# A planned transformer block: ScalarE planned at a shorter pitch, ten x tiles transposed by DMA, slabs and wo loaded after them

## The chip, the cores and the metric

The kernel runs on one core of a Trainium2 chip. The time is device microseconds of one launch. Before the change it is 1136.66 us, the median of three runs from 1135.99 to 1137.84.

## What is computed

One transformer block on 2048 tokens of width 1024, in bf16: attention with 32 query heads of 32 columns that share one key head and one value head, then a gated feed-forward of width 3584.

```python
x = A_x                                   # (1, 2048, 1024)
n = layernorm(x)                          # (x - m) / sqrt(v + eps)
q = heads(n @ wq); k = n @ wk; v = n @ wv # q: 32 heads of 32; k, v: 32 columns
p = softmax(q @ k.T * 32 ** -0.5)
h = x + merge(p @ v) @ wo
m = layernorm(h)
out = h + (sigmoid(m @ w_gate) * (m @ w_up)) @ w_down
```

## The kernel before, in words

**A planner writes the order.** The kernel is straight-line code for five in-order engines. While it is built, `Plan` (from line 40) simulates the engines with fixed costs and lists each engine's instructions in the order in which its simulation starts them; `emit` then writes these lists with semaphore waits. On the chip the order never changes: an instruction that is ready later than planned holds everything behind it on its engine. `op` (58) adds an instruction; for PE it is placed at once, for the others `step` (94) takes the earliest that can start, by priority where several can. Costs planned: a matmul of n columns n/2.4 + 2.4 ns, 97 ns for each change of PE between dense, row-tiled ("row": scores) and column-tiled ("col": PV, SUM) matmuls (`SWITCH`, 151), ACT `t_act` (143), DVE `t_dve` (147), a DMA 450 ns of SP and a landing from a rate and fixed parts (116 to 121). "pace" spaces the weight loads at `PACE_RATE`.

**The stages.** x comes in 16 tiles of 128 tokens into `ring`. Of each tile DVE takes the statistics and subtracts the mean (359), POOL makes 1/std (340 to 346), DVE or ACT scales it into `xn` (`make_norm1`, 363), PE transposes it in eight 128x128 blocks into PSUM (`mk_xT`, 398), and `evac` (257) gives the copy into `xnT`, a part of `zone`, to ACT (266) or DVE (267), whichever is free sooner by the plan. KV groups (438) make keys and values; Q groups (491, 507) make queries, which go through DRAM. When a tile quad of x is scaled, its room in `ring` is given to the first gate and up slabs (`load_next`, 847); a slab is 1024 x 512 of w_gate or w_up, 1 MB in four DMAs. wo is loaded at line 310, after x and wq.

A score visit (`emit_S`, 614) handles one half of a 128-token tile's heads (`hf`, 0 to 31) against 128 keys (`kt`): four S matmuls (row-tiled), then two exps of 128x1024 on ACT (632), which write one slot of 2048 columns. There are 512 visits. The first 32 go over halves 0 and 1 alternately and need the keys of tile after tile as these come. DVE adds the slots of a half up (607); SUM (657) gives the denominators, by DRAM, to all partitions (670, 671); PV (693) multiplies by the values. For halves 0 and 1 (`RAW`) the denominators come from PV-like matmuls with ones. `finish` (678) divides. OP (776) multiplies by wo, DVE adds x (783), takes statistics and normalises (789), and a DMA transposes the result into `hnT` (804).

The feed-forward goes tile by tile: GU groups (gate: tanh on ACT, 919; up: combined on DVE, 925), seven slab pairs a pass, odd passes backwards so that two slab pairs are reused; then D groups (949, four quarters of the width) with w_down, which stays in SBUF as 14 loads (`load_wd`, 472) into `zone`, in the room of xnT and wq. So a wd load waits for the last use of its x block, and the last six wait for all of Q (`wd_after_q`, 485). GU of tile 1 and any D wait for all of Q too.

**How the next PE work is picked** (main loop, from 1001). If a score visit can start and ACT's backlog is below `run`, it goes first, also in the middle of a group. Else the current group goes on. A long group (D, GU, Q) may be set aside for a PV, SUM or OP group. If there is no current group, the first class in `PRIO` (380) with a ready group and a free one of the two PSUM banks is taken; `PRIO_D` (379) takes its place when a D group is due. PV and SUM are let in from row mode, or with few free slots (`in_row`, 654; `pv_few`, `sum_few`).

Of the kernel before, what the change touches and what calls it, by code (L numbers as in the profile page):

```python
# [10 lines left out]
ALU = mybir.AluOpType  # L11

P = 128
DH = 32
LN_EPS_BF16 = 1.0013580322265625e-05
SEM = 75.0


TUNE = dict(nkn=2, few=0, rmin=1000, hmin=3, h0=100, h1=100, hf=1.5, run=1300, sum_few=12, pv_few=1, d_off=0,
            d_a=1, d_b=1, eb=0, eq=0)  # L20

# [18 lines left out]
class Plan:  # L40


    ENG = ("act", "dve", "pool", "sp")
    DMA_RATE = 260.0
    LATE = {"rb": 1000.0, "hT0": 300.0, "hT1": 300.0}
    PACE_RATE = 250.0

# [46 lines left out]
    def step(self, limit):  # L94
        best = None
        for e in self.ENG:
            h = self.heap[e]
            if h:
                s = min(self.start_of(o) for o in h)
                if best is None or s < best[0]:  # L100
                    best = (s, e)
        if best is None or (limit is not None and best[0] > limit):
            return False
        s, e = best
        h = self.heap[e]
        o = min((o for o in h if self.start_of(o) <= s + 1e-9), key=lambda o: (o.prio, o.seq))
        h.remove(o)
        if o.pace and self.pace_free > s:
            s2 = self.pace_free
            prev = [a for a in self.lists["act"][-6:] if a.end <= s2]  # L110
            if prev:
                o.deps.append(prev[-1])
            s = s2
        self.free[e] = s + o.occ
        o.start = s
        if o.nbytes:
            if o.pace:
                self.pace_free = s + o.nbytes / self.PACE_RATE
            go = max(s + 1300.0, self.dma_free)
            self.dma_free = go + o.nbytes / self.DMA_RATE  # L120
            o.end = self.dma_free + 700.0 + self.LATE.get(o.key, 0.0)
        else:
            o.end = s + o.lat
        o.pos = len(self.lists[e])
        self.lists[e].append(o)
        for u in o.users:
            u.ready = max(u.ready, o.end)
            u.missing -= 1
            if u.missing == 0:
                self.heap[u.eng].append(u)  # L130
        o.users = []
        return True
# [10 lines left out]
def t_act(n):  # L143
    return dict(occ=n / 1.2 + 96.0, lat=n / 1.2 + 186.0 + SEM)

# [8 lines left out]
def bass_sequential_preLN__grouped_kv_mqa__glu_gated_glu__prompt_kernel(  # L154
# [12 lines left out]
    Bsz, S, D = A_x.shape  # L167
# [17 lines left out]
    with ExitStack() as es:  # L185
# [58 lines left out]
        def x_sb(t):  # L244
            return x_ring[:, t, :]
# [63 lines left out]
        load_wq(3)  # L309
        wo_ld = dma(lambda: SP.dma_start(wo_sb[:, :, :], A_wo.rearrange("(g p) n -> p g n", p=P)), "wo", D * D * 2, prio=1)  # L310

# [39 lines left out]
        sv1 = {}  # L351
        for tiles in ([0], [1], [2, 3], [4, 5], [6, 7], [8, 9, 10], [11, 12, 13], [14, 15]):
            r = stats(0, tiles, [x_sb(t) for t in tiles], [[x_ld[t]] for t in tiles], 3)
            for t in tiles:
                sv1[t] = r
        xnorm = {}
        xcent = {}
        for t in range(NT):
            xcent[t] = pl.op("dve", lambda t=t: DVE.tensor_scalar(  # L359
                out=x_sb(t), in0=x_sb(t), scalar1=mvr[:, 0, t, 0:1], scalar2=None, op0=ALU.subtract),  # L360
                [sv1[t][0]], prio=2, occ=330, lat=500)

        def make_norm1(t, deps):
            dst, src, sc = xn[:, t % 2, :], x_sb(t), rstd[:, 0, t:t + 1]
            xnorm[t] = evac(lambda: ACT.activation(out=dst, in_=src, func=ACTF.Copy, scale=sc),
                            lambda: DVE.tensor_scalar(out=dst, in0=src, scalar1=sc, scalar2=None, op0=ALU.mult),  # L366
                            1024, [xcent[t], sv1[t][1]] + deps, 1, 3.2, bias=TUNE["eb"])

        make_norm1(0, [])
# [9 lines left out]
        PRIO_D = ["xT", "KV", "Q0", "PV", "SUM", "OP", "hT", "D", "GU", "Q1", "Q"]  # L379
        PRIO = ["xT", "KV", "Q0", "PV", "SUM", "OP", "hT", "Q1", "Q", "GU", "D"]  # L380

# [13 lines left out]

        xT_ev = {}

        def mk_xT(t):
# [6 lines left out]
            def after(b, last):  # L405
# [3 lines left out]
                if t + 2 < NT:  # L409
                    make_norm1(t + 2, [last])  # L410
                    if (t + 2) % 4 == 3:
                        sl = (t + 2) // 4
                        load_next([(ring_u[:, u], [xnorm[2 * u], xnorm[2 * u + 1]]) for u in (2 * sl, 2 * sl + 1)])
                queue_after_xT(t)
                return [xT_ev[t]]
# [172 lines left out]
        late_adds = collections.defaultdict(list)  # L588
        RAW = (0, 1)
        rs_b = h_sb[:, 2, :].bitcast(F32)  # L590
# [23 lines left out]
        def emit_S(v):  # L614
# [23 lines left out]
            if hh == 1 and c % 2 == 1 and kt == NT - 1:  # L638
                pair_last_S[c // 2] = last
                load_q(c // 2 + 2)  # L640
            if kt % 8 == 7:
                if kt == NT - 1 and hf not in RAW:
                    queues["SUM"].append(mk_SUM(hf))
                queues["PV"].append(mk_PV(hf, kt // 8))
                if hf in RAW:
                    queues["PV"].append(mk_PV(hf, kt // 8, True))

        rb_ld = {}
        rs_ev = {}
# [28 lines left out]
        def finish(hf):  # L678

            if hf not in rb_ld or (hf, 1) not in oun_ev:  # L680
                return
            c, hh = hf // 2, hf % 2
            o = oun[:, hf % 2, :]
            r = rs_b if hf == 1 else rb[:, :]
            ot_ev[hf] = pl.op("dve", lambda: DVE.tensor_tensor(
                out=OT[:, 4 * hh:4 * hh + 4, :], in0=o.rearrange("p (a b) -> p a b", a=4),
                in1=r.rearrange("p (a b) -> p a b", a=4), op=ALU.mult),
                [oun_ev[(hf, 1)], op_last.get(c - 1)] + rb_ld[hf], prio=0, occ=600, lat=690)
            if hh == 1:
# [3 lines left out]
        def mk_PV(hf, part, sums=False):  # L693

            kts = range(8 * part, 8 * part + 8)

# [6 lines left out]
            def after(b, last):  # L703
                if sums:
                    r = rs_b if hf == 1 else rb[:, :]
                    if part == 0:
# [3 lines left out]
                    e = pl.op("dve", lambda: DVE.tensor_tensor(out=r, in0=F_ps[:, b, :], in1=r, op=ALU.add),  # L710
                              [last, rs_ev[hf]], prio=0, **t_dve(512))
                    rb_ld[hf] = [pl.op("dve", lambda k=k: DVE.reciprocal(r[:, k * P:(k + 1) * P], r[:, k * P:(k + 1) * P]),
                                       [e], prio=1, occ=P * 8 / 0.96 + 20, lat=P * 8 / 0.96 + 90 + SEM) for k in range(4)]
# [7 lines left out]
                else:  # L721
                    oun_ev[(hf, 1)] = pl.op("dve", lambda: DVE.tensor_tensor(out=o, in0=F_ps[:, b, :], in1=o, op=ALU.add),  # L722
                                            [last, oun_ev[(hf, 0)]], prio=0, **t_dve(512))
                    finish(hf)
                return [oun_ev[(hf, part)]]
# [50 lines left out]
        def mk_OP(t, dc):  # L776
# [19 lines left out]
            def gate():  # L796
                return t in xr_ld and xr_ld[t].end is not None and (t == 0 or (t - 1) in hT_last)
            return Group("OP", atoms, lambda: [ot_ev[2 * t], ot_ev[2 * t + 1], wo_ld], after, gate)

# [145 lines left out]

        ND = 4
        DW = D // ND

        def mk_D(p, t, dq):
# [9 lines left out]
            def after(b, last):  # L959
# [5 lines left out]
                d_ev[t].append(e)  # L965
                if dq % 2 == 1:
                    dc = dq // 2
                    s2 = slice(dc * 512, (dc + 1) * 512)
                    out_dma[(t, dc)] = dma(lambda: SP.dma_start(of[t * P:(t + 1) * P, s2], h_sb[:, t % NHB, s2]),
                                           f"o{t % NHB}{dc}", P * 1024, d_ev[t][-2:], prio=2)  # L970
                if dq == ND - 1 and t + NHB < NT:
                    load_xr(t + NHB)
                return [e]
            return Group("D", atoms, lambda: [hact_ev[(t, ft)] for ft in order[:-8]] + [wd_ld.get(ft) for ft in order[:-8]], after,
                         lambda: q_left[0] == 0)

        d_ev = collections.defaultdict(list)
        for t in range(NT):
            queues["xT"].append(mk_xT(t))

# [20 lines left out]
        while True:  # L1001
# [10 lines left out]
            if 1 in ot_ev and 0 in xr_ld and 2 not in xr_ld:  # L1012
                load_xr(2)
            start_ffn()
            if v < NV:
# [5 lines left out]
                if can_s and run - t < TUNE["run"]:  # L1021
# [3 lines left out]
                    idle = 0  # L1025
                    continue
            else:
                can_s = False
            if cur is not None and not held and cur[0].cls in LONG and known(bank_rel[1 - cur_b], t) and (
                    v >= NV or len(free_slots) <= TUNE["few"] or (len(cur[1]) - cur_i) * max(25.0, cur[1][cur_i][1] / 2.4 + 2.4) >= TUNE["rmin"]):  # L1030

                for cl in ("PV", "SUM", "OP", "hT"):
                    if queues[cl]:
                        gr = queues[cl][0]
# [24 lines left out]
            else:  # L1059
                pick = None  # L1060
                banks = [b for b in range(2) if known(bank_rel[b], t)]
                if banks:
                    pr = PRIO
                    if d_due and len(queues["GU"]) <= d_due[0] + TUNE["d_off"]:
# [135 lines left out]
```

## Time and profile before

| what | us |
|---|---|
| median of the runs | 1136.66 |
| the profiled execution, its own time | 1136.12 |
| its span, first to last instruction | 1134.3 |
| PE busy | 1095.5 (97%) |
| PE weight loads busy | 747.4 (66%) |
| ACT busy | 1033.6 (91%) |
| DVE busy | 834.9 (74%) |
| mean granted TensorE clock | 0.994 |
| DMA moved | 218.13 MB, 192 GB/s mean |

How to read it: busy PE is matmuls in flight, and they overlap, so the engine's real use is read from the distances between starts. ACT's exps overlap too (1035 ns each, but they start closer than that). In rows of the profile "xN" is a count, and what stands in brackets is idle time before an instruction and what ended it. A span is shorter than the execution's own time by what lies around the first and last instruction, here 1.8 us.

### The profile page before, as it was taken

How to read it: one execution, taken by the hardware profiler on the slowest of the kernel's cores; microseconds unless marked ns; L12 is line 12 of the kernel's file. 1: busy time of each engine (PE TensorE's matmuls, PEld its weight loads, DVE VectorE, ACT ScalarE, POOL GpSimd, SP SyncE). 2: the span in 40 equal slices, each digit the busy share in tenths (PEclk: the TensorE clock that was granted, in tenths of full speed). 3: DMA queues.
4: the chain of work that ended last, by engine and by line, in shares of the span. 5: the costliest groups of instructions: out<-in, count | busy, mean ns of one | idle time of the engine just before them, and what ended most of it. 6: DMA issues, size and time to landing. Idle time of an engine off the chain costs nothing.

```text
span 1134.3 us, 34513 instructions
## 1 busy us (share of the span) xinstructions
PE 1095.5 (97%) x15085; PEld 747.4 (66%) x15112; DVE 834.9 (74%) x1042; ACT 1033.6 (91%) x1157; POOL 55.6 (5%) x94
## 2 busy tenths in 40 slices
PE   5999989799999999999999999999999999999999
PEld 4643355467676776767676676767677676667798
DVE  8838987597877767787777877787777778777521
ACT  5899999999999999999999999999999999999410
POOL 4200000010000000000000000000000100000000
PEclk9999999899999999999999999999999999999999
DMA  9423379565766767666667576665847475666783
GB/s 311 146 82 119 98 253 257 176 192 175 194 187 208 213 204 201 182 179 193 196 187 227 153 245 184 180 206 166 255 129 232 144 245 147 213 199 187 241 278 106
DMA packets 231671, 218.13 MB, mean 192 GB/s; under 512 B 34784, under 2 KB 218080, under 8 KB 231520
## 3 DMA queue, kind: packets, MB, share of 16 engines
q1 hardware_dynamic: 231520, 215.92, 63.7%
q8 instruction: 119, 1.95, 0.7%
q14 instruction: 32, 0.26, 0.1%
HBM read 203.55 MB, written 8.11 MB: 187 GB/s over the span
## 4 chain that ended last, share of the span: by engine, by line
PE 87%; ACT 6%; DVE 5%; issue 1%; DMA 1%; POOL 0%; DVEq 0%
PE F_ps L383 74%; PE S_ps L383 13%; ACT Pr L632 5%; DVE st L327 1%; DVE st L329 1%; DVE acc L607 1%; DVE zone L366 1%; DMA ring<-in_B_w_gate_dram 1%; DVE zone L267 1%; DVE ring L359 0%; ACT tnh L919 0%; DVE hact L925 0%; DMA ring<-in_A_x_dram 0%; PE F_ps L401 0%; DVE oun L722 0%
## 5 line engine op out<-in xcount | busy, mean ns | idle before, releaser
L632 ACT ACTIVATE Pr<-S_ps 128x1024 bf16<-128x1024 f32 x1008 | 964.2, 1035 | 20.4 <-PE S_ps L383 11.5
L607 DVE TENSOR_TENSOR acc<-acc,Pr 128x2048 bf16<-128x2048 bf16 x420 | 513.5, 1223 | 103.2 <-ACT Pr L632 91.9
L383 PE MATMUL F_ps<-hnT,ring 128*128 128x128 bf16 x6848 | 440.2, 220 | 3.9 <-issue 1.8
L383 PEld LDWEIGHTS F_ps<-hnT,ring 128*128 128x128 bf16 x6848 | 387.7, 98 | 75.7 <-issue 70.0
L383 PE MATMUL F_ps<-zone,hact 128*128 128x256 bf16 x1792 | 227.8, 273 | 0.0
L383 PE MATMUL S_ps<-QTb,kT 32*128 32x512 bf16 x2048 | 203.2, 387 | 12.3 <-ACT Pr L632 11.2
L383 PEld LDWEIGHTS F_ps<-zone,hact 128*128 128x128 bf16 x1792 | 163.4, 98 | 48.6 <-issue 29.8
L383 PE MATMUL F_ps<-Pr,Vt 128*32 128x512 bf16 x2016 | 132.7, 387 | 1.6 <-DVE r_sb L668 0.6
L383 PEld LDWEIGHTS S_ps<-QTb,kT 32*128 32x128 bf16 x2048 | 51.7, 91 | 115.6 <-ACT Pr L632 46.7
L919 ACT ACTIVATE tnh<-F_ps 128x512 f32<-128x512 f32 x112 | 67.4, 601 | 51.3 <-PE F_ps L383 50.4
L925 DVE SCALAR_TENSOR_TENSOR hact<-tnh,F_ps 128x512 bf16<-128x512 f32 x112 | 76.4, 682 | 45.8 <-PE F_ps L383 43.9
L383 PEld LDWEIGHTS F_ps<-Pr,Vt 128*32 128x32 bf16 x2016 | 45.7, 97 | 59.4 <-issue 18.2
L383 PE MATMUL F_ps<-zone 128*128 128x512 bf16 (+3 forms) x575 | 73.8, 276 | 2.7 <-ACT zone L266 1.4
L383 PE MATMUL F_ps<-wo_sb,OT 128*128 128x512 bf16 x238 | 59.7, 381 | 1.6 <-DVE h_sb L783 0.6
L383 PEld LDWEIGHTS F_ps<-zone 128*128 128x128 bf16 x584 | 40.3, 99 | 29.9 <-issue 8.9
L340 POOL TENSOR_SCALAR zb<-mvb 128x1 bf16<-128x1 bf16 (+2 forms) x24 | 9.1, 381 | 1022.7 <-DVE mvb L336 1022.5
L962 DVE SCALAR_TENSOR_TENSOR h_sb<-F_ps,h_sb 128x256 bf16<-128x256 f32 x64 | 26.9, 420 | 31.2 <-PE F_ps L383 31.0
L607 DVE TENSOR_TENSOR acc<-Pr 128x2048 bf16<-128x2048 bf16 x30 | 35.9, 1198 | 10.3 <-ACT Pr L632 10.2
L383 PEld LDWEIGHTS F_ps<-wo_sb,OT 128*128 128x128 bf16 x256 | 22.5, 98 | 27.7 <-issue 7.2
L722 DVE TENSOR_TENSOR oun<-F_ps,oun 128x512 f32<-128x512 f32 x32 | 22.0, 687 | 24.3 <-PE F_ps L383 24.2
L668 DVE RECIPROCAL r_sb<-F_ps 128x64 f32<-128x64 f32 x30 | 16.7, 556 | 21.9 <-PE F_ps L383 21.7
L783 DVE TENSOR_TENSOR h_sb<-F_ps,h_sb 128x512 bf16<-128x512 f32 x32 | 22.1, 690 | 10.8 <-PE F_ps L383 10.2
(72 smaller groups left out, 333.9 us busy)
## 6 DMA issues: line engine op xcount, KB each, us to landing
ring<-in_B_w_gate_dram SPq DMA_DIRECT2D x312, 256.0 KB, 3.8
ring<-in_B_w_up_dram SPq DMA_DIRECT2D x312, 256.0 KB, 3.9
rb<-r_scratch SPq DMA_DIRECT2D x120, 64.0 KB, 2.3
zone<-in_B_w_down_dram SPq DMA_DIRECT2D x14, 512.0 KB, 4.5
ring<-in_A_x_dram SPq DMA_DIRECT2D x16, 256.0 KB, 6.5
h_sb<-in_A_x_dram SPq DMA_DIRECT2D x16, 256.0 KB, 2.8
out_dram<-h_sb SPq DMA_DIRECT2D x32, 128.0 KB, 3.5
Pr<-in_B_w_up_dram SPq DMA_DIRECT2D x16, 256.0 KB, 4.1
```

The costliest lines, as they stand in the source:

```text
L267: lambda: DVE.tensor_copy(out=out_ap, in_=in_ap))
L327: a = pl.op("dve", lambda s=s, src=src: DVE.bn_stats(st[:, s, 0, :], src[:, 0:512]), dp, prio=prio, occ=600, lat=756, order=[st_user.get(s)])
L329: b = pl.op("dve", lambda s=s, src=src: DVE.bn_stats(st[:, s, 1, :], src[:, 512:1024]), dp, prio=prio, occ=600, lat=756, order=[st_user.ge ...
L383: return lambda: PE.matmul(o, lhsT=l, rhs=r, start=start, stop=stop, **kw)
L607: add_op[(hf, kt)] = pl.op("dve", lambda: DVE.tensor_tensor(out=a, in0=in0, in1=slot, op=ALU.add), dp, prio=6, **t_dve(2048, 1.92))
L632: exps[u] = pl.op("act", lambda i=i, pb=pb: ACT.activation(out=slot[:, i * 1024:(i + 1) * 1024].rearrange("p (a b) -> p a b", a=2), in_=S_ ...
L668: rc = pl.op("dve", lambda: DVE.reciprocal(r_sb[:, :], F_ps[:, b, 0:64]), [last, rd_ld.get(hf - 1)], prio=0, occ=64 * 8 / 0.96 + 20, lat=6 ...
L722: oun_ev[(hf, 1)] = pl.op("dve", lambda: DVE.tensor_tensor(out=o, in0=F_ps[:, b, :], in1=o, op=ALU.add), [last, oun_ev[(hf, 0)]], prio=0, ...
L783: h_ev[(t, dc)] = pl.op("dve", lambda: DVE.tensor_tensor(out=h_sb[:, t % NHB, sl], in0=F_ps[:, b, :], in1=h_sb[:, t % NHB, sl], op=ALU.add ...
L919: box["a"] = pl.op("act", lambda: ACT.activation(out=tnh[:, :], in_=F_ps[:, b, :], func=ACTF.Tanh, scale=0.5), [last, box.get("e")], prio= ...
L925: e = pl.op("dve", lambda: DVE.scalar_tensor_tensor(out=ho, in0=shape(tnh[:, :]), scalar=1.0, in1=shape(F_ps[:, b, :]), op0=ALU.add, op1=A ...
L962: e = pl.op("dve", lambda: DVE.scalar_tensor_tensor(out=h_sb[:, t % NHB, sl], in0=F_ps[:, b, 0:DW], scalar=0.5, in1=h_sb[:, t % NHB, sl], ...
```

## The change

The costs that the planner reckons with: ACT is occupied for n/1.2 + 58 ns by an instruction of n columns, not + 96. A DMA is planned as 1500 ns, its bytes at 270 (not 260) per ns, and 750 ns; extra lateness is 300 for rb, 400 for hT and xt (before 1000 and 300). Weight loads are paced at 280, not 250.

x tiles 0 to 5 go on as before. Tiles 6 to 15 are scaled in place by DVE and transposed by DMA straight into `xnT` (`x_by_dma`). All slabs, and wo, are loaded only after tile 15 has been transposed. Statistics are grouped in pairs.

The order of PE: GU and D stand ahead of Q1 and Q. D waits for all of w_down. GU's gate waits for three of a slab's four DMAs. SUM is let in from row mode or with at most 2 free slots (before 12), PV with 3 (before 1). In column mode, when the next visit is ready within 200 ns, PE waits. The planner's evacuation choice is biased against ACT (`eb` 450, `eq` 1000). Other new keys have values that leave things as they are (`parts=2`, `raw=2`, `nd=4`, and `pc=16`, which is no tile).

```diff
-TUNE = dict(nkn=2, few=0, rmin=1000, hmin=3, h0=100, h1=100, hf=1.5, run=1300, sum_few=12, pv_few=1, d_off=0,
-            d_a=1, d_b=1, eb=0, eq=0)
+TUNE = dict(swait=200, parts=2, raw=2, rl=0, nd=4, pc=16, rate=270, pace=280, xd=6, qf=0, dall=1, wo_late=1,
+            nkn=3, few=2, rmin=700, hmin=1, h0=100, h1=100, hf=1.0, run=900, sum_few=2, pv_few=3, d_off=2,
+            d_a=0, d_b=1, eb=450, eq=1000)
...
-    LATE = {"rb": 1000.0, "hT0": 300.0, "hT1": 300.0}
+    LATE = {"rb": 300.0, "hT": 400.0, "xt": 400.0}
...
-            go = max(s + 1300.0, self.dma_free)
-            self.dma_free = go + o.nbytes / self.DMA_RATE
-            o.end = self.dma_free + 700.0 + self.LATE.get(o.key, 0.0)
+            go = max(s + 1500.0, self.dma_free)
+            self.dma_free = go + o.nbytes / TUNE["rate"]
+            o.end = self.dma_free + 750.0 + self.LATE.get(o.key.rstrip("0123456789"), 0.0)
...
-    return dict(occ=n / 1.2 + 96.0, lat=n / 1.2 + 186.0 + SEM)
+    return dict(occ=n / 1.2 + 58.0, lat=n / 1.2 + 186.0 + SEM)
...
-        wo_ld = dma(lambda: SP.dma_start(wo_sb[:, :, :], A_wo.rearrange("(g p) n -> p g n", p=P)), "wo", D * D * 2, prio=1)
+        wo_lds = []
+
+        def load_wo():
+            wo_lds.append(dma(lambda: SP.dma_start(wo_sb[:, :, :], A_wo.rearrange("(g p) n -> p g n", p=P)), "wo", D * D * 2,
+                              [xT_ev[NT - 1]], prio=1))
...
+        def x_by_dma(t):
+
+            xnorm[t] = pl.op("dve", lambda: DVE.tensor_scalar(
+                out=x_sb(t), in0=x_sb(t), scalar1=rstd[:, 0, t:t + 1], scalar2=None, op0=ALU.mult),
+                [xcent[t], sv1[t][1]], prio=1, occ=330, lat=500)
+            xT_ev[t] = dma(lambda: SP.dma_start_transpose(xnT[:, t // 4, :, (t % 4) * P:(t % 4 + 1) * P], x_sb(t)),
+                           f"xt{t}", P * D * 2, [xnorm[t]], prio=0)
+            ring_free(t)
+            queue_after_xT(t)
+            if t == NT - 1:
+                load_wo()
+
+        def ring_free(t):
+            if t == NT - 1:
+                load_next([(ring_u[:, u], [xnorm[2 * u], xnorm[2 * u + 1], xT_ev[t]] + [xT_ev[k] for k in (2 * u, 2 * u + 1)])
+                           for u in range(2 * NSLAB)])
...
-        PRIO = ["xT", "KV", "Q0", "PV", "SUM", "OP", "hT", "Q1", "Q", "GU", "D"]
+        head = ["xT", "KV", "Q0", "PV", "SUM", "OP", "hT"]
+        PRIOS = [head + ["GU", "D", "Q1", "Q"], head + ["Q1", "Q", "GU", "D"], head + ["Q1", "GU", "Q", "D"]]
...
-            return Group("D", atoms, lambda: [hact_ev[(t, ft)] for ft in order[:-8]] + [wd_ld.get(ft) for ft in order[:-8]], after,
+            return Group("D", atoms, lambda: [hact_ev[(t, ft)] for ft in order[:-8]] + [wd_ld.get(ft) for ft in (order if TUNE["dall"] else order[:-8])], after,
...
+                if pl.pe_mode == "col" and sd is not None and not can_s and not (
+                        cur is not None and cur[1][cur_i][2] != "dense") and known(sd, t + TUNE["swait"]) and run - t < TUNE["run"] + TUNE["swait"]:
+
+                    pl.free["pe"] = t + 25.0
+                    continue
...
-            if cur is not None and not held and cur[0].cls in LONG and known(bank_rel[1 - cur_b], t) and (
-                    v >= NV or len(free_slots) <= TUNE["few"] or (len(cur[1]) - cur_i) * max(25.0, cur[1][cur_i][1] / 2.4 + 2.4) >= TUNE["rmin"]):
+            if cur is not None and not held and cur[0].cls in LONG and known(bank_rel[1 - cur_b], t):
 
                 for cl in ("PV", "SUM", "OP", "hT"):
-                    if queues[cl]:
+                    if queues[cl] and (v >= NV or len(free_slots) <= TUNE["few"] or cl == "PV" and pl.pe_mode == "row" or (
+                            len(cur[1]) - cur_i) * max(25.0, cur[1][cur_i][1] / 2.4 + 2.4) >= TUNE["rmin"]):
```

## The prediction

> **What bounds the kernel now.** I read the windows first, then the order of matmuls in the stretch where they dip, then the groups. The windows (PE, PEld, DVE, ACT, POOL busy; granted clock; DMA share; GB/s):
>
> ```profile
> 160.00:170.00 10.00, 7.84 (x102) 4.39 (x104) 8.27 (x9) 10.00 (x13) 0.00 (x0) 1.00 0.81 253
> 180.00:190.00 10.00, 8.17 (x125) 3.99 (x123) 7.78 (x9) 8.04 (x11) 0.00 (x0) 0.83 1.06 259
> 210.00:220.00 10.00, 3.20 (x26) 0.64 (x24) 4.31 (x4) 10.00 (x12) 0.00 (x0) 0.63 0.68 207
> 300.00:400.00 100.00, 99.04 (x1431) 68.78 (x1429) 78.48 (x92) 98.82 (x111) 5.07 (x6) 1.00 0.65 185
> 1060.00:1134.30 74.30, 70.62 (x991) 63.92 (x990) 19.16 (x33) 7.91 (x13) 1.34 (x3) 1.00 0.66 204
> ```
>
> From 300 us on PE and ACT both look full. Which is the bound is told by the distance between score visits (one visit: four S matmuls, two exps). Near 130 us with filler work they start 1.94 us apart; in the dip at 210 us, with none, they follow ACT alone:
>
> ```profile
> 128.43 0.40 PE L383 MATMUL S_ps<-QTb,kT 32*128 32x512 bf16 x4
> 130.37 0.39 PE L383 MATMUL S_ps<-QTb,kT 32*128 32x512 bf16 x4
> ...
> 200.44 2.18 PE L383 MATMUL F_ps<-hnT,ring 128*128 128x128 bf16 x36
> ...
> 207.76 1.26 PE L383 MATMUL F_ps<-zone,hact 128*128 128x256 bf16 x10
> 208.95 0.40 PE L383 MATMUL S_ps<-QTb,kT 32*128 32x512 bf16 x4
> 209.28 0.94 PE L383 MATMUL F_ps<-zone,hact 128*128 128x256 bf16 x7
> 210.47 0.39 PE L383 MATMUL S_ps<-QTb,kT 32*128 32x512 bf16 x4 [0.26 <-ACT Pr L632]
> 212.30 0.40 PE L383 MATMUL S_ps<-QTb,kT 32*128 32x512 bf16 x4 [1.44 <-ACT Pr L632]
> 214.14 0.61 PE L383 MATMUL S_ps<-QTb,kT 32*128 32x512 bf16 x4 [1.44 <-ACT Pr L632]
> 215.97 0.61 PE L383 MATMUL S_ps<-QTb,kT 32*128 32x512 bf16 x4 [1.22 <-ACT Pr L632]
> 217.80 0.61 PE L383 MATMUL S_ps<-QTb,kT 32*128 32x512 bf16 x4 [1.22 <-ACT Pr L632]
> 219.64 0.61 PE L383 MATMUL S_ps<-QTb,kT 32*128 32x512 bf16 x4 [1.22 <-ACT Pr L632]
> ```
>
> (219.64 - 212.30)/8 gives 917 ns per exp, the real pitch of ACT; 1.94 us is PE's own doing, so ACT has about 5% to spare and PE is the bound. The same rows give PE's prices: a gate/up matmul every (2.18 - 0.22)/35 = 56 ns, a down matmul every (1.26 - 0.27)/9 = 110 ns, 0.33 us from an S start to the next dense matmul.
>
> Taking every matmul start in the trace in order, and from each distance the normal one of its kind, the span of 1134.3 is: 9.6 before the first matmul, 959.9 of work, 119.0 for 1151 changes between dense, S and column-tiled matmuls (PV, SUM), 42.7 of waits, 3.1 after the last start. The 512 visits need 1024 of the changes; 127 are extra. The waits lie so: 8.6 before 60 us, 1.9 in 60 to 150, **19.1 in 150 to 225**, 12.1 in 225 to 1060, 1.1 after. The 19.1 have two parts. D of tile 0 starts at 206 and sits on PE unfinished from 210 until 223.6: the last of 14 wd loads is issued only at 213.97, behind slab loads on SP, and lands some 4.5 us later. That is 9.9 (the last 1.5 of it PV at half the clock after the idling, the 0.63 above). The other 9.2 are GU of tile 0 waiting for slabs while Q, done at 143, can no longer fill in; DMA moves 121 GB/s in 100 to 150 and 310 in 150 to 160.
>
> **The change, part by part.**
>
> *Shorter ACT pitch* (949 to 911 ns planned for 1024 columns; backlog 1300 to 900). The real pitch is 917. The S phase can end near 17 + 1024 x 0.917 + 112 x 0.48 (tanh, from start distances) + 6 = 1016 instead of 1060, with the dense work pushed behind it. But PE's total stays: the same matmuls, the same 512 visits. Alone: 0. It can lose if PE now waits for ACT: the plan is 6 ns per exp too quick, at most 1024 x 6 ns = 6 us; but a real visit costs PE about 15 ns more than the plan charges (317 ns from last S to dense against 302), which keeps PE the later one. Here the Trainium skill speaks against the change: "ScalarE: Activation LUTs", section "What happens when an exp ACTIVATE runs", gives 186 ns + 0.833 ns per column for one with immediates and an overlap of 93 back to back, so 946 ns here, almost the old plan. By that, ACT needs 1024 x 29 ns = 30 us more than by the row, in a plan that expects it earlier: +30 of waits, so a slower kernel. The row decides: five visits in a queue, 917. I take 0, from -2 to +6.
>
> *Ten tiles by DMA.* PE loses 80 transposes x 56 ns = 4.5 us. DVE or ACT loses ten evacuations (671 or 1028 ns). Normalising was on DVE for all sixteen and stays. Added: ten DMA transposes. First the tile that the kernel already transposes so (issue time on SP, then time to landing), then the PE path's groups:
>
> ```profile
> L804 SPq DMA_TRANSPOSE hnT<-hn x16: 1240/1270/2291, 122.9 to 1086.0; - x16
> ...
> DMA to landing us min/median/max: 3.0/3.6/5.4
> ```
> ```profile
> L401 PE MATMUL F_ps<-ident,zone 128*128 128x128 bf16 x128 | 10.7, 231 | 11.7 <-DVE zone L366 9.8 <-ACT QTb L266 0.7 <-DVE hact L267 0.6
> L267 DVE COPY zone<-F_ps 128x1024 bf16<-128x1024 bf16 x12 | 8.0, 671 | 0.6 <-PE F_ps L401 0.6
> ```
>
> A tile by PE takes 0.62 + 0.67 us plus hand-overs, by DMA 3.6: 2 us later each, but pipelined. The ten issues hold SP 10 x 1.27 = 12.7 us, where the plan charges 0.45 each: 8 us of drift over some 25 us; behind them on SP stand Q stores, early wd loads and the deferred slabs, none due then. DVE, full until 40 us, sets the tiles' pace (about 16 x 2.75 us); relieved of up to six copies (4 us), but given ACT's Q evacuations by the new biases (7 x 0.40), it ends about 1 us sooner, which the longer path eats. Here too a rule speaks against: "VectorE: DVE Perf Modes", "The three transpose paths" and its rules, prices a 128x128 block at 390 ns on TensorE and 1309 ns by DMA and prefers TensorE. Serially that would be 8 x 1.31 = 10.5 us a tile, not 3.6, and ten tiles 105 us; the row measures just such eight-block tiles, so 3.6 stands. Head: 0, bounds -4 and +4 by the 8.6 us of waits there.
>
> *Slabs and wo later.* Issued after tile 15, about 50 us, instead of 15.7 and 18. The first 4 MB of slabs and 2 MB of wo at 270 GB/s land by about 75. Their first users before stand at 143 (GU) and 109.9 (OP); GU may come about 25 us earlier, still behind. Hidden: 0; uncovered it would cost the landing times, 4 to 14 us.
>
> *GU and D ahead of Q; D waits for all of wd; DMA planned at 1500 ns + 270 GB/s + 750; pace 280.* GU(0) can start when hT(0) is there, near 115 instead of 143. Its ten streamed slabs (3.7 us each at 270 GB/s) then run beside the 18.6 us of Q left at 113 (86 matmuls x 216 ns), and the DMA's idle share before 150 is used. Part two of the stall, 9.2: bounds 0 and 9; I take 5, since wd's last six loads still need Q's end, now later. D(0) no longer parks on PE unfinished; GU(1), whose first four slabs lie in SBUF, runs in its place. Part one, 9.9: bounds 5 and 10; I take 9.
>
> *Mode rules* (SUM from S mode or with at most 2 free slots, PV from 3, waiting up to 200 ns in column mode instead of going dense). Each extra change is about 100 ns, a wait of up to 200 buys two. 127 to perhaps 105: -2, bounds -6 and +2. Behind a waiting PE stand only its own matmuls; ACT has its backlog.
>
> *Rest of the waits* (225 to 1060, mostly around SUM): the DMA constants now lie nearer the rows (hT 3.62 planned, 3.6 measured), but r_sb through DRAM is planned 0.2 sooner in sum and DVE gets denser: 0, bounds -4 and +4. The tail grows to about 95 us and needs 10 MB per 41 us of PE, 250 GB/s; the last but one of the 40 slices shows 278 without waits, so 0.
>
> Sum: -4.5 - 9 - 5 - 2 = -20.5; span 1113.8. The profiled execution took 1136.12, 1.8 more than its span, and stands 0.5 under the median: **1116**.
>
> **Rivals.**
> - *The starvation only moves.* Q's later end delays wd 8 to 13 (3 MB, 11 us) and GU(1) waits for its slabs instead. For it: 310 GB/s at 150, share over 1. Against: idle DMA before. Then -4.5 - 2 and a third of the stall: 1136.7 - 6.5 - 6 = 1124 (1120 to 1132).
> - *Slower: the DMA transposes set the head.* Scores 0 to 31 need the keys of every tile in order, and with them Q of later blocks. If in the head's full DMA (354 to 372 GB/s, share 1.1) each transpose takes 5.4 us and they do not overlap, tile 15 comes at 27 + 54 = 81 instead of 48; PE has Q of blocks 0 and 1 and S for part of it, and loses some 25. 1136.7 - 20.5 + 25 = 1141. It decides from 2 us of PE idling per transposed tile on. Against: with slabs and wo gone the loads are in by about 23 us (last issue at 15.2, 7.6 to landing).
> - *More is won*: both parts of the stall whole, half the extra changes, a third of the 12.1: -4.5 - 19 - 6 - 4 gives 1103.
>
> **How the numbers follow.** Mine 0.50 (1108 to 1120), moved starvation 0.22, more won 0.14, slower (with ACT as bound) 0.14. What a measurement here tells from no change is about 0.2%, 2.3 us. Slower holds 0.12, 0.04 lies inside 0.2% (parts of two cases), faster 0.84. Range 1102 to 1132: the bounds of D(0), the slabs and the modes, and the moved starvation.
>
> **What would show it.** Right: no stretch after 100 us with PE under 9 of 10 and a clock under 1; D(0) uninterrupted; GU from about 115; 48 transposes on PE; S ending at 1015 to 1030; ACT still waiting for PE. Wrong: L401 or key matmuls waiting on DMA zone in 25 to 60 us; S waiting on ACT all along; gaps at PE while slabs land late after 1020; more than 1151 mode changes.

## The result and the profile after

The changed kernel takes 1126.2 us, the median of four runs (1121.68 to 1126.95), beside 1136.45 before on the same chip: a ratio of 0.990, with a 95% interval from 0.9872 to 0.9927. The forecast was 1116 in a range of 1102 to 1132: the direction held, and about half of the expected 20 us came.

The windows after, in the stretches that were shown of before and around the new dip (PE, PEld, DVE, ACT, POOL busy; granted clock; DMA share; GB/s):

```profile
160.00:170.00 10.00, 10.00 (x137) 5.99 (x134) 9.67 (x11) 10.00 (x12) 0.00 (x0) 1.00 0.96 296
180.00:190.00 10.00, 5.81 (x102) 2.27 (x98) 9.01 (x14) 10.00 (x12) 2.24 (x3) 0.84 0.97 259
190.00:200.00 10.00, 8.73 (x98) 5.61 (x98) 6.50 (x7) 8.39 (x10) 0.00 (x0) 0.64 0.55 167
210.00:220.00 10.00, 10.00 (x133) 6.36 (x130) 4.57 (x6) 10.00 (x13) 0.00 (x0) 1.00 0.71 223
300.00:400.00 100.00, 99.16 (x1415) 68.22 (x1412) 80.83 (x95) 99.20 (x113) 6.47 (x6) 1.00 0.61 178
```

The dips at 160 and 210 are gone, but there is one at 183 to 191, again with PE idle; behind it, from 188 to 196, the granted clock is 0.50. The steady part, 300 to 400, looks no better than before. The account of PE, made as in the prediction (the 27 matmuls of before that the trace lacks are filled in from their weight loads here, so a few numbers differ slightly from the ones there):

| us | before | after |
|---|---|---|
| before the first matmul | 9.8 | 9.8 |
| work at normal distances | 960.7 | 955.8 |
| changes between dense, S and column mode (number) | 119.5 (1156) | 116.6 (1126) |
| waits, 0 to 60 | 8.6 | 7.8 |
| waits, 60 to 150 | 1.2 | 3.3 |
| waits, 150 to 225 | 18.8 | 9.6 |
| waits, 225 to the end | 12.8 | 17.9 |
| after the last matmul's start | 3.0 | 2.9 |
| span | 1134.3 | 1123.8 |

So 4.9 came from work, 2.9 from mode changes, 9.2 from the starved stretch and 0.8 from the head, and 7.2 were given back in two other places: 2.1 between 60 and 150 us, and 5.1 in small waits after 225 us.

**The new dip.** The order of events in the changed kernel's timeline:

```profile
174.22 0.97 SPq L503 DMA_DIRECT2D zone<-in_B_w_down_dram  x2
...
177.77 7.77 SPq L503 DMA_DIRECT2D zone<-in_B_w_down_dram  x5
...
179.84 0.69 DVE L819 TENSOR_TENSOR h_sb<-F_ps,h_sb 128x512 bf16<-128x512 f32 x1
...
183.03 1.12 POOL L344 TENSOR_SCALAR zb<-mvb 128x1 bf16<-128x1 bf16 x1 [65.05 <-DVE mvb L340]
...
185.52 0.55 DVE L825 TENSOR_SCALAR hn<-h_sb,mvr,rstd 128x1024 bf16<-128x1024 bf16 x1 [0.33 <-DVE r_sb L699]
...
186.90 1.32 SPq L840 DMA_TRANSPOSE hnT<-hn  x1
187.04 0.61 PE L410 MATMUL S_ps<-QTb,kT 32*128 32x512 bf16 x4 [1.44 <-ACT Pr L662]
188.26 0.57 SPq L503 DMA_DIRECT2D zone<-in_B_w_down_dram  x1
188.88 0.61 PE L410 MATMUL S_ps<-QTb,kT 32*128 32x512 bf16 x4 [1.22 <-ACT Pr L662]
190.71 0.61 PE L410 MATMUL S_ps<-QTb,kT 32*128 32x512 bf16 x4 [1.22 <-ACT Pr L662]
...
191.88 0.80 PE L410 MATMUL F_ps<-hnT,ring 128*128 128x128 bf16 x6 [0.56 <-DMA hnT<-hn]
```

Q's last matmul ends at 174.2 and GU of tile 0 at 181. D of tile 0 needs w_down, whose last eight loads are issued only from Q's end on, 174 to 188; GU of tile 1 needs that tile's hT, which starts with h at 179.8 and lands at 191.8. Until then PE has visits alone, at ACT's pace.

**The small waits.** Once a tile, at 13 places over the whole steady part, PE stood 0.1 to 0.8 us between D and GU (8.0 us in all), and some 0.28 between S and SUM (3.6 in all). One such place, POOL, DVE and PE together:

```profile
497.88 1.23 DVE L637 TENSOR_TENSOR acc<-acc,Pr 128x2048 bf16<-128x2048 bf16 x1
497.94 1.28 POOL L344 TENSOR_SCALAR zb<-mvb 128x1 bf16<-128x1 bf16 x1 [60.26 <-DVE mvb L340]
...
499.21 1.23 DVE L637 TENSOR_TENSOR acc<-acc,Pr 128x2048 bf16<-128x2048 bf16 x1
499.31 1.54 POOL L347 TENSOR_TENSOR dsb<-zb,cst 128x1 bf16<-128x1 bf16 x1
...
500.93 0.55 POOL L350 TENSOR_TENSOR rstd<-dsb,cst 128x1 f32<-128x1 bf16 x1
...
501.57 0.55 DVE L825 TENSOR_SCALAR hn<-h_sb,mvr,rstd 128x1024 bf16<-128x1024 bf16 x1 [1.14 <-POOL rstd L350]
502.03 0.69 DVE L757 TENSOR_TENSOR oun<-F_ps,oun 128x512 f32<-128x512 f32 x1
...
502.82 0.89 PE L410 MATMUL F_ps<-hnT,ring 128*128 128x128 bf16 x13 [0.67 <-issue]
...
503.76 0.42 DVE L998 SCALAR_TENSOR_TENSOR h_sb<-F_ps,h_sb 128x256 bf16<-128x256 f32 x1
...
504.24 0.42 PE L410 MATMUL F_ps<-acc,sel 128*32 128x64 bf16 x32 [0.21 <-DVE h_sb L998]
```

DVE stands 1.14 us at hn, which waits for POOL's rstd; oun behind it empties the PSUM bank that GU needs, and GU starts 0.1 us after oun ends. The trace says "issue" for GU's wait; that it waits for the bank is read from the order, and the first experiment below tries it. SUM waits in the same way for the bank that D's last evacuation (h_sb) empties. POOL is late because DVE's adds (acc) run beside it. The group of zb, first before, then after:

```profile
L340 POOL TENSOR_SCALAR zb<-mvb 128x1 bf16<-128x1 bf16 x18 | 7.8, 432 | 999.3 <-DVE mvb L336 999.1
```
```profile
L344 POOL TENSOR_SCALAR zb<-mvb 128x1 bf16<-128x1 bf16 x18 | 18.6, 1035 | 969.2 <-DVE mvb L340 969.0
L825 DVE TENSOR_SCALAR hn<-h_sb,mvr,rstd 128x1024 bf16<-128x1024 bf16 x16 | 8.7, 546 | 16.4 <-POOL rstd L350 16.0 <-DVE r_sb L699 0.3
```

Taken singly, in both kernels from 100 us on, zb lasts about 220 ns where no add is under way when it starts, and 1115 to 1281 where one is; then it ends 78 to 120 ns after that add. The Trainium skill states this in "SBUF — State Buffer", section "SBUF: two separate sides": POOL and a DVE instruction with two SBUF inputs share a port pair under an exclusive lock, and the later one waits for all of the other. The trace agrees, with the numbers just given; the planner reckons 330 ns.

### The profile page after: what moved, and what is told of

It is laid out like the page before. It is cut to its first block, busy times and chain, and to the rows that moved or that the text cites. A ratio compares the mean times of both kernels' runs of the same rounds, so it can differ in the third digit from the quotient of the medians.

```text
span 1123.8 us, 34582 instructions
## 1 busy us (share of the span) xinstructions
PE 1089.5 (97%) x15032; PEld 737.6 (66%) x15032; DVE 827.8 (74%) x1040; ACT 1013.0 (90%) x1151; POOL 69.4 (6%) x97
## 4 chain that ended last, share of the span: by engine, by line
PE 36%; ACT 28%; DVE 18%; issue 8%; POOL 4%; DMA 4%; SPq 1%; DVEq 0%
PE F_ps L410 31%; ACT Pr L662 26%; DVE acc L637 9%; PE S_ps L410 5%; ACT tnh L955 2%; DMA rb<-r_scratch 2%; POOL dsb L347 2%; DVE st L331 2%; POOL zb L344 2%; DVE st L333 2%; DVE hact L961 1%; DVE h_sb L819 1%; SPq L702 1%; POOL rstd L350 1%; DVE h_sb L998 1%
## 5 line engine op out<-in xcount | busy, mean ns | idle before, releaser
L662 ACT ACTIVATE Pr<-S_ps 128x1024 bf16<-128x1024 f32 x1008 | 950.2, 1053 | 19.9 <-PE S_ps L410 17.6
L410 PE MATMUL F_ps<-hnT,ring 128*128 128x128 bf16 x6720 | 430.3, 220 | 7.6 <-issue 7.0
L410 PEld LDWEIGHTS F_ps<-hnT,ring 128*128 128x128 bf16 x6720 | 382.5, 98 | 67.0 <-issue 61.1
L410 PE MATMUL F_ps<-zone,hact 128*128 128x256 bf16 x1792 | 233.7, 273 | 0.0
L410 PEld LDWEIGHTS F_ps<-zone,hact 128*128 128x128 bf16 x1792 | 160.0, 98 | 57.8 <-issue 42.0
L410 PE MATMUL F_ps<-Pr,Vt 128*32 128x512 bf16 x2016 | 127.1, 381 | 0.0
L410 PE MATMUL F_ps<-zone 128*128 128x512 bf16 (+3 forms) x584 | 76.7, 276 | 4.9 <-DVE Vt L266 2.1
L344 POOL TENSOR_SCALAR zb<-mvb 128x1 bf16<-128x1 bf16 (+1 forms) x25 | 20.2, 807 | 989.7 <-DVE mvb L340 989.5
L410 PE MATMUL F_ps<-wo_sb,OT 128*128 128x512 bf16 x256 | 63.3, 380 | 0.7 <-DVE h_sb L998 0.4
L347 POOL TENSOR_TENSOR dsb<-zb,cst 128x1 bf16<-128x1 bf16 (+1 forms) x25 | 29.8, 1195 | 1.9
```

The source lines that it names most:

```text
L344: f = pl.op("pool", lambda: POOL.tensor_scalar(out=zb[:, ph, tk], in0=mvb[:, ph, tk, 1], scalar1=LN_EPS_BF16, scalar2=None, op0=ALU.add), ...
L347: g = pl.op("pool", lambda: POOL.tensor_tensor(out=dsb[:, ph, tk], in0=zb[:, ph, tk], in1=half[:, 0:k], op=ALU.pow), [f, c0], prio=prio - ...
L410: return lambda: PE.matmul(o, lhsT=l, rhs=r, start=start, stop=stop, **kw)
L662: exps[u] = pl.op("act", lambda i=i, pb=pb: ACT.activation(out=slot[:, i * 1024:(i + 1) * 1024].rearrange("p (a b) -> p a b", a=2), in_=S_ ...
```

## The experiments

Theory A: PE's work and its waits set the time, and the loss against the forecast is DVE standing at hn. The last start of an S matmul is called the end of the S phase. Measured:

| kernel | median us | ratio to before (95%) | S phase ends | PE work | waits |
|---|---|---|---|---|---|
| before | 1136.45 | 1 | 1059 | 960.7 | 41.4 |
| after | 1126.2 | 0.990 (0.9872 to 0.9927) | 1038 | 955.8 | 38.7 |
| hn one place later | 1120.69 | 0.9861 (0.9843 to 0.9878) | 1036 | 956.3 | 35.5 |
| hn three places later | 1118.03 | 0.9843 (0.9824 to 0.9862) | 1030 | 955.8 | 30.7 |
| before, new pitch alone | 1135.97 | 0.9997 (0.9985 to 1.001) | 1019 | 957.9 | 43.4 |
| after, old pitch | 1153.36 | 1.0151 (1.013 to 1.0173) | 1068 | 955.9 | 67.8 |
| after, PE transposes | 1135.28 | 0.999 (0.9981 to 0.9999) | 1023 | 960.4 | 41.0 |
| after, Q first | 1125.98 | 0.9907 (0.9892 to 0.9923) | 1031 | 956.2 | 38.5 |
| after, Q first, old pitch | 1145.49 | 1.0077 (1.0051 to 1.0103) | 1063 | 956.7 | 53.0 |
| after, D not waiting for all of w_down | 1124.4 | 0.989 (0.9872 to 0.9907) | 1026 | 956.2 | 33.1 |
| after, old pitch, PE transposes | 1151.1 | 1.0131 (1.0116 to 1.0146) | 1062 | 960.6 | 58.0 |
| after, old DMA rate and pace | 1130.68 | 0.9948 (0.9929 to 0.9966) | 1031 | 956.3 | 42.1 |

Each is compared with runs of the kernel before on its own chip (medians 1136.45 to 1137.25). PE work and waits are those of the traced execution, which for "hn one place later" is 2.6 us above its median and for "after, old pitch" 4.6 above. Except in the two hn runs, the planner makes a new order each time, so a few us of such a difference can be the order's own.

**hn one place later.**

```diff
         pl.drain()
         pl.stall = stall
+        row = pl.lists["dve"]
+        for o in [o for o in row if o.tag is not None and o.tag[0] == "hn" and 2 <= o.tag[1] <= 14]:
+            i = row.index(o)
+            row[i:i + 2] = [row[i + 1], o]
```

> The changed kernel with one swap in DVE's list per tile 2 to 14: hn (the second layernorm's result, which waits for POOL's rstd) goes behind the oun evacuation that followed it. PE's order is untouched. Theory A (the new steady waits of some 0.6 us at D to GU and 0.28 at S to SUM come from DVE standing at hn while POOL is held up by adds): both vanish in 13 tiles, 6 to 11 us less than the changed kernel's 1126, so 1115 to 1120. Rival B (GU waits there for a slab, or the bank is late anyway): within 2 us of 1126.

1120.69: 0.7 above A's range and far from B's. In the trace the D to GU waits, 8.0 us at 13 places, are gone. Those at S to SUM are still there, 4.0 us at 13 places, so that half of the expectation was wrong: they had another cause on the same engine. And new waits have come, between GU and OP: 4.5 us at six places, 1.2 at four in the changed kernel. There DVE, which hn no longer holds, stands at OT until rb (the denominators) has landed, and D's last evacuation behind it is late.

**hn three places later.**

```diff
-            row[i:i + 2] = [row[i + 1], o]
+            row[i:i + 4] = row[i + 1:i + 4] + [o]
```

> As the run with hn one place later in DVE's list, but three places later: behind oun, the next add and D's last evacuation, which frees the bank that SUM waits for. PE's order is untouched. Theory A (the remaining 0.3 to 0.5 us at S to SUM, 4 us in 13 tiles, come from DVE reaching that evacuation late): 2 to 4 us under the run with one place, so 1117 to 1119. Rival B (SUM's wait is set by the add's own length, planned 1135 ns and measured 1221): within 1 us of that run, 1120.

1118.03: A. The same place in this kernel's timeline:

```profile
497.69 0.69 DVE L757 TENSOR_TENSOR oun<-F_ps,oun 128x512 f32<-128x512 f32 x1 [0.33 <-PE F_ps L410]
497.86 0.55 POOL L350 TENSOR_TENSOR rstd<-dsb,cst 128x1 f32<-128x1 bf16 x1
...
499.11 0.89 PE L410 MATMUL F_ps<-hnT,ring 128*128 128x128 bf16 x13
499.44 0.42 DVE L998 SCALAR_TENSOR_TENSOR h_sb<-F_ps,h_sb 128x256 bf16<-128x256 f32 x1
499.77 0.54 DVE L825 TENSOR_SCALAR hn<-h_sb,mvr,rstd 128x1024 bf16<-128x1024 bf16 x1
499.93 0.39 PE L410 MATMUL S_ps<-QTb,kT 32*128 32x512 bf16 x4
500.26 0.42 PE L410 MATMUL F_ps<-acc,sel 128*32 128x64 bf16 x32
```

PE goes from D to GU and from S to SUM without a gap, at all 13 places of each. POOL is as slow as before (zb 1.28); in these tiles nobody waits for it any more. PE's order is the changed kernel's, so the 8 us between 1126.2 and 1118.0 belong to the place of hn on DVE (the intervals of the two ratios don't meet; those of the two hn runs do, so the step between them rests on the trace). This is the fastest kernel of the study.

What PE still waits after 225 us is mostly one more instruction of this kind. At nine places, 5.5 us in all, PE stands before OP or inside GU, and each time DVE has stood 1.1 to 2.3 us at OT shortly before. Its waits for rb in the whole span, in the kernel before, the changed one and this one (us, times, longest):

```profile
DVE OT L685 <- DMA rb<-r_scratch: 4.7, 5, 1.7
DVE OT L716 <- DMA rb<-r_scratch: 10.6, 13, 1.8
DVE OT L716 <- DMA rb<-r_scratch: 24.7, 22, 2.3
```

The change lowered rb's planned lateness from 1000 to 300 ns, so OT is planned sooner; no run puts that number back, so that this is the reason is not shown.

**The pitch alone, in the kernel before.**

```diff
-    return dict(occ=n / 1.2 + 96.0, lat=n / 1.2 + 186.0 + SEM)
+    return dict(occ=n / 1.2 + 58.0, lat=n / 1.2 + 186.0 + SEM)
```

> The kernel before with only ACT's planned occupancy changed, + 58 instead of + 96 ns. Theory A (PE's total is the bound, the planned pitch only moves work behind the S phase): 1136, give or take 4 for a re-dealt order; the D(0) stall near 210 stays. Rival B (the pitch carries the gain): about 1126 or less.

1135.97, ratio 0.9997: A. The S phase ends 40 us sooner, the dense work behind it is 40 us longer, and the sum is the same. PE still waits 17 us in 150 to 225, so the stall near 210 stayed.

**The old pitch in the changed kernel** (the same line, the other way).

> The changed kernel with ACT's planned occupancy put back to + 96 ns. Theory A: 1126, give or take 4. Rival B (with visits spaced as before, feed-forward work runs out in the S phase and PE idles, so that the pitch is worth most of the change): 1136 or more, with idle PE at GU all through the S phase.

1153.36: B, by a wide margin, and slower than the kernel before. Windows of this kernel:

```profile
500.00:600.00 100.00, 94.39 (x1304) 61.78 (x1308) 79.36 (x94) 98.44 (x109) 3.59 (x6) 1.00 0.50 153
700.00:800.00 100.00, 96.74 (x1320) 63.39 (x1315) 77.84 (x93) 97.73 (x110) 3.60 (x6) 1.00 0.48 145
1060.00:1100.00 40.00, 30.75 (x467) 23.83 (x465) 21.37 (x27) 13.64 (x17) 1.34 (x3) 0.98 0.94 282
```

PE has holes in the S phase (27 us of waits in 225 to 1000, against 11 before), and in the tail GU waits for slabs at a DMA share of 0.94:

```profile
1079.35 2.25 PE L410 MATMUL F_ps<-hnT,ring 128*128 128x128 bf16 x32 [0.59 <-DMA ring<-in_B_w_gate_dram]
1082.59 0.49 PE L410 MATMUL F_ps<-hnT,Pr 128*128 128x128 bf16 x6 [0.99 <-DMA Pr<-in_B_w_up_dram]
```

So theory A held for the old order of PE and fell for the new one. A second form of it: at the old planned pitch the planned visits, not PE's work, hold the end of the S phase near 1060, and PE work taken out turns into waiting. The next two runs try this and a rival reason.

**Old pitch and PE transposes**, `xd=15` beside the old line.

> The changed kernel with ACT's planned occupancy at + 96 and fifteen x tiles transposed by PE. Theory A (at the old planned pitch the visits, not PE's total, set the end of the S phase near 1065, so that PE work taken out turns into waiting): 4.6 us more PE work costs nothing, 1149 to 1156 like the run with the old pitch alone, and PE waits less than the 67.8 us of that run. Rival B (PE's total counts at the old pitch too): 1158 or more, as the PE transposes cost 9 us at the new pitch.

1151.1: A. With 4.7 us more PE work the time is no longer; PE waits 58.0 instead of 67.8 (about half of this difference is that the other kernel's traced execution lay 4.6 us above its median). But this kernel has the PE work and the planned pitch of the kernel before (960.6 and 960.7 us of work) and is 14.5 us slower, so the savings on PE are not what makes the old pitch dear: something in the new order is.

**Q first, and Q first at the old pitch**, `qf=1`.

> The changed kernel with Q1 and Q ahead of GU and D in the order of classes, as before the change. Theory A (GU ahead of Q took the slab waits of 150 to 180 away): GU of tile 0 waits for slabs again, some 8 us more in 60 to 225, 1130 to 1136. Rival B (that the waits there are set by the attention of tile 1 and by wd alone): 1126, give or take 3.

1125.98: the time says B, the order of Q and GU is worth nothing in sum. A's mechanism is there all the same: from 150 to 180 PE waits some 6.5 us instead of 0.2, in pauses inside GU of tile 0 as in the kernel before. But the dip behind it shrinks (some 6 instead of 9.4 from 180 to 225), so the stretch 150 to 225 has 12.6 instead of 9.6, of 18.8 before, and 225 to the end gives that back (14.6 instead of 17.9).

> The changed kernel with both put back: Q ahead of GU, and ACT's planned occupancy + 96. Theory A (the old pitch costs 27 us only because GU ahead of Q lets the feed-forward catch up with the attention, so that GU is run at the DMA's pace with nothing to fill in): the cost of the old pitch shrinks to under 10, 1132 to 1142. Rival B (it is the other rules of the new order, or the short PE total, that make the old pitch dear): 1150 or more.

1145.49: neither. The old pitch costs 19.5 us with Q first (from 1125.98) and 27.2 with GU first, so GU running ahead explains some 8 of the 27. The traces show where: at the old pitch PE waits about 16 us after 1000 us with GU first and about 3 with Q first (the slab waits of the tail are gone), while the holes between 225 and 1000 stay, 27 and about 26. Why the new order at the old pitch is 9 us slower than the kernel before, which has that pitch too, is not settled: the PV, SUM and wait rules differ, and they were not undone singly.

**PE transposes**, `xd=15` at the new pitch.

> The changed kernel with fifteen x tiles transposed by PE and only the last by DMA, slabs and wo still loaded after the last tile. Theory A: nine more tiles x 8 x 56 ns = 4 us more PE work, and a head as slow as before: 1130, give or take 4. Rival B (the DMA transposes are what delays the head): below 1124. A third outcome, over 1136, would mean that the regular order of the changed kernel hangs on the short head.

1135.28, between A's range and the third outcome: 9 us, of which the account shows 4.6 of work, 2.3 of mode changes (1150 instead of 1126) and 2.3 of waits. The first is the transposes themselves. The rest goes with another order: the changed kernel's repeats from tile to tile (D begins every 63 to 64 us), this one's doesn't (16 to 71). That the shorter head is what lets it repeat was not tried.

**D not waiting for all of w_down**, `dall=0`.

> The changed kernel with D allowed to start before all of w_down has landed, as before the change. Theory A (the wait of tile 1's hT would be the same, D fills part of it and then parks PE): 1126 to 1134, with D of tile 0 interrupted between 183 and 192. Rival B (D waiting for all of w_down is what leaves PE empty at 183 to 191): 1120 or less.

1124.4: neither. It is 1.6 under A's range and 4.4 above the rival's, and no further from the changed kernel than their intervals reach. What A described is in the trace: D of tile 0 begins at 185, and from 189 to 194 only four of its matmuls run, until the last w_down load has landed. But it costs nothing: PE's waits in 150 to 225 are 7.7 instead of 9.6. The new rule on w_down gains nothing here.

**Old DMA rate and pace**, `rate=260, pace=250`.

> The changed kernel with the planner's DMA rate and the pace of weight loads put back to 260 and 250. Theory A (the waits left in 150 to 225 are those of tile 1's attention and of wd, which comes later at the slower pace: 8 loads x 0.2 us): 1126 to 1132, waits in 150 to 225 of 9 to 13 us. Rival B (the faster stream of slabs is what took half of that stretch's waits away): those waits return to 17 to 20 us and the time to 1134 or more.

1130.68: A. Waits in 150 to 225 are 11.6. In every kernel of the table PE waits between 7.7 and 18.8 us in that stretch; no edit tried here removes it.

## Why the prediction was right and wrong

- *What bounds the kernel*: PE, and ACT's real pitch of 917: right. In the changed kernel's waits, PE's S matmuls wait for ACT 4.8 us in all, five times, most of it in the dip. The S phase ended at 1038, though, not between 1015 and 1030.
- *Pitch alone 0*: right where it was worked out, in the order of before (0.9997). But the term was taken as independent of the others, and it is not: without it the rest of the change gives 1153. Nine tiles' transposes less on PE are worth 9 us at the new pitch and nothing at the old one; the prediction gave both ends of the S phase, 1060 and 1016, and drew from them only that work moves behind it. That end alone does not set the time, though: it is 1059 in the kernel before and 1063 with Q first at the old pitch, which is 9 us slower. The estimate of 946 ns from the Trainium skill's "ScalarE: Activation LUTs" (the figures stand in its section "What ACT_TABLE_LOAD costs") does not fit: visits with nothing between them again follow every 1.83 us, 917 an exp.
- *Transposes -4.5*: right in size (4.9 in the account). *Head 0*: -0.8. The ten DMA transposes took 3.3 us to landing (median); nothing of the slower rival showed:

```profile
zone<-ring SPq DMA_TRANSPOSE x10, 3.3
```

- *Slabs and wo later, 0*: no slab or wo wait is seen for it; GU of tile 0 came at 124, not 115. PE waits 3.3 instead of 1.2 between 60 and 150, the largest 1.3 us at 142, with DVE held 1.6 at OT by rb's landing just before. Whether that comes from rb's planned lateness or from this order was not tried.
- *D(0) -9 and slabs -5*: came as -9.2 together, not -14. The slab waits of 155 to 195 are gone nearly whole, and D of tile 0 no longer parks. The step that failed is "GU(1), whose first four slabs lie in SBUF, runs in its place": slabs were not GU(1)'s last input, hT of tile 1 was, at 191.8. The rival "the starvation only moves" was right here, with another cause than it named: wd was late as it said, but GU(1) waited for the attention of tile 1, not for slabs. And the reason given for the gain, GU ahead of Q, carries only 3 of the 9.2 in sum; the new DMA rate and pace carry 2.0 (11.6 without them), the new rule on w_down none. What brings the rest was not singled out.
- *Mode rules -2*: -2.9, 1126 changes of 1156.
- *Rest of the waits 0, bounds -4 and +4*: this step failed, by +5.1. It weighed DMA constants; the wait came from POOL's chain, of which the prediction priced nothing at all in the steady part, though the profile of before has it: 432 ns a zb, and DVE at hn 1.1 us at worst. The hn runs show it. The DMA constants may come next: what is left with hn moved is OT standing for rb.

Sum: -20.5 forecast, -10.5 in the span. Of the 10 missing, 7.2 are waits that the change brought and 4.8 the dip that moved; 2 came in more than forecast elsewhere. The measured 1126.2 lies outside 1108 to 1120, the prediction's own case, and inside 1120 to 1132, its rival's; that it lies in the whole range is in part luck, since half of what was missing came from a wait that no case named.

## What to carry to other kernels

In a program whose order is fixed ahead, one instruction that is planned too early on an in-order engine holds up all that stands behind it: look for the short wait that comes once a tile, at the engine that releases PSUM banks, and when one is gone, look for the next in the same list. Ask of each saving on PE whether PE will then be the bound; a saving and the pacing that lets it count are one term, not two (here nine tiles' transposes: 9 us or nothing). When a stall is taken away at one consumer, list the inputs of what is to run instead, and when each lands.

## What was not expected of the hardware

A POOL instruction on a 128x1 column takes 220 ns alone and up to 1281 beside a DVE add of 128x2048, and a power 570 and about 1550: the add's end, not POOL's own work, sets it. A change from S to dense matmuls costs PE 111 ns beyond the normal distance (317 from the last S start, where PV matmuls of the same 512 columns follow after 206), from dense to S 96 (152 after a matmul of 128 columns, whose normal distance is 56), before as after, while the planner charges 97 for both.
